# Retention and a bilinear FFN on one core: another order of the tokens, and the third pair in the opening's form

## The chip, the core and the metric

The kernel runs on one core of a Trainium2 chip. The metric is the device time of one execution in microseconds (us). "Median" is the median of the runs named.

TensorE is PE in the profile, its weight loads are PEld, VectorE is DVE, ScalarE is ACT, GpSimd is POOL, and SyncE (SP) issues most transfers.

## The reference, cut to what matters

```python
B, H, S, D = 8, 8, 576, 64                     # 4608 tokens, 512 features
scores = (q @ k.T) / sqrt(D)                   # per batch and head
ret    = scores * gamma_h ** (i - j), 0 where j > i
attn   = ret @ v                               # -> x [4608, 512]
out    = ((x @ w_a) * (x @ w_b)) @ w_out       # d_ff = 1536
```

The decay lets a block of 64 tokens be computed from its own scores and one running state (the sum of k^T v over the earlier blocks of the batch). A batch has nine blocks of 64. Tokens can be worked off in any order as long as the states of a batch come in sequence; each token's FFN row is independent of the others.

## The kernel before

Attention is cut into units that are dropped into gaps between the FFN's matrix products, because the FFN (1,404 products, mostly of 512 columns, 0.216 us each) fills TensorE from about 18 us to the end. There are three forms:

- the *opening*: 512 tokens as 2 pairs of 256 tokens x 2 halves of four heads. A partition holds two neighbouring tokens (512-byte rows in the loads), and the products use the array in quarters of 64x64;
- two single 128-token *chunks* (the third pair, tokens 512 to 767), with 256-byte rows;
- fifteen *pairs* of 256 tokens in quarters, each worked in a *stretch*: outputs from states, a fence (a small ScalarE copy out of the output tile, for which the products that add to this tile must wait), state products (`keyed`), scores (`matched`), outputs from scores.

```python
    def rows_of(i):                      # tokens of chunk i: batches one after the other
        b, m = 2 * (i // PER), i % PER   # PER = 9 chunks for two batches
        if m < MID:
            return [(0, 128, b, 128 * m)]
        if m == MID:                     # this one straddles two batches
            return [(0, 64, b, 128 * m), (64, 64, b + 1, 0)]
        return [(0, 128, b + 1, 64 + 128 * (m - MID - 1))]

    def keyed(n):                        # state products of a stretch
        kvs = [ps_ffn.tile([128, 2, HP, 64], FP32, tag="ab", name=f"kv{a}")
               for a in (0, 1)]          # two of the four PSUM buffers of the FFN
        ...
                for a, r in QUADS:
                    if block_of(n, 2 * kp + a) == BL - 1:
                        continue         # a batch's ninth block feeds no state
                    nc.tensor.matmul(kvs[a][half(r), kp, c, :], ...)
        def add(i):                      # running sums on VectorE
            ...
            elif m < BL - 1:
                nc.vector.tensor_tensor(sums[:, i], own, prev, op=ALU.add)
        later.append(lambda: (add(0), add(1)))   # one entry runs in each gap
        later.append(lambda: (add(2), add(3)))

    def stretch(into, outof):
        flush()
        if outof is not None:
            ...
            from_states(outof, o, begun)
            nc.scalar.copy(fence, o[:, :, 0, kp, 0])   # before from_keys may add
        if into is not None:
            convert, convert_swapped = keyed(into)
            masked = matched(into)
        if outof is not None:
            scaled = from_keys(outof, o, begun)
        ...

    # the last lines of ffn_block: one store for 128 tokens
                    nc.sync.dma_start(out[rows, cols], osb[:, cols])

    # places, counted in FFN products of 512 columns
    for i, places in ((4, (110, 117, 121, 127)), (5, (127, 132, 136, 139))):
        todo += [(at, one_by_one, (what, i))           # the two single chunks
                 for at, what in zip(places, "CTSA")]  # cast, turn, score, output
```

Of the kernel before, what the change touches and what calls it, by code (L numbers as in the profile page):

```python
# [18 lines left out]
def kernel(  # L19
# [21 lines left out]

    NP = NTOK // 256
    BL = S // 64
    FIRST = 3
    PER = 2 * S // 128
    MID = PER // 2
    HALF = S - 128 * MID
    assert HALF == 64 and NTOK % (2 * S) == 0 and BL == 9

    def rows_of(i):  # L50

        b, m = 2 * (i // PER), i % PER
        if m < MID:
            return [(0, 128, b, 128 * m)]
        if m == MID:
            return [(0, 64, b, 128 * m), (64, 64, b + 1, 0)]
        return [(0, 128, b + 1, 64 + 128 * (m - MID - 1))]

# [54 lines left out]
    staged, shared = {}, {}  # L113
# [7 lines left out]

    def load(i):
        tiles = []
        for name, src in (("qf", q), ("kf", k), ("vf", v)):
            t = half_of(stage, i, [DM], FP32, name)
            for r0, n, b, s0 in rows_of(i):
                nc.sync.dma_start(
                    t[r0:r0 + n, :].rearrange("p (h d) -> p h d", h=H),
                    src[b, :, s0:s0 + n, :].rearrange("h s d -> s h d"))
            tiles.append(t)  # L130
        staged[i] = tiles
# [3 lines left out]
    def load_pair(n):  # L135
        if n >= NP:
            return
        paired[n] = []
        for name, src in (("qf", q), ("kf", k), ("vf", v)):
            t = stage.tile([128, 2 * DM], FP32, tag=name, name=name + "2")  # L140
            for kp in (0, 1):
                for r0, m, b, s0 in rows_of(2 * n + kp):
                    nc.sync.dma_start(
                        t[r0:r0 + m, kp * DM:(kp + 1) * DM]
                        .rearrange("p (h d) -> p h d", h=H),
                        src[b, :, s0:s0 + m, :].rearrange("h s d -> s h d"))
            paired[n].append(t)

    def load_step(n, hh, which):

        if n not in paired:
            paired[n] = [stage.tile([128, 2 * DM], FP32, tag=name, name=name)
                         for name in ("qf", "kf", "vf")]
        nc.sync.dma_start(  # L154
            paired[n][which][:, hh * DM:(hh + 1) * DM]
            .rearrange("p (h e) -> p h e", h=4),
            (q, k, v)[which][0, 4 * hh:4 * hh + 4, 256 * n:256 * n + 256, :]
            .rearrange("h (p two) d -> p h (two d)", two=2))

    STEPS = [(0, 0), (1, 0), (0, 1), (1, 1)]  # L160
# [7 lines left out]
    idxp_i = const.tile([128, 6], INT32)  # L168
    nc.gpsimd.iota(idxp_i[:, 0:4], pattern=[[256, 2], [1, 2]], base=0,
                   channel_multiplier=2)  # L170
    for col, base in ((4, 512), (5, 64)):
        nc.gpsimd.iota(idxp_i[:, col:col + 1], pattern=[[1, 1]], base=base,
                       channel_multiplier=1)
# [12 lines left out]
    idxv_i = const.tile([128, BL, 2], INT32)  # L186
    mask = const.tile([128, 128], BF16)
    mask2 = const.tile([128, 128], BF16)
    mask3 = const.tile([128, 64], BF16)

    def make_masks():
        nc.gpsimd.memset(two_states, 0.0)
        nc.gpsimd.iota(idxv_i, pattern=[[256, BL], [128, 2]], base=0,
                       channel_multiplier=1)
        nc.gpsimd.memset(mask, 1.0)
        nc.gpsimd.affine_select(
            out=mask, in_=mask, compare_op=ALU.is_ge, fill=0.0,
            base=0, pattern=[[1, 128]], channel_multiplier=-1)
        nc.gpsimd.tensor_copy(mask2, mask)
        nc.gpsimd.memset(mask2[0:64, 64:128], 0.0)  # L200
# [3 lines left out]
    idxp_f = const.tile([128, 6], FP32)  # L204
    nc.vector.tensor_copy(idxp_f, idxp_i)
    nc.vector.tensor_scalar_add(idxp_f[64:128, 4:5], idxp_f[64:128, 4:5],
                                -float(S))
# [6 lines left out]
    vs = const.tile([128, H, 6], FP32)  # L214
# [4 lines left out]
    qs = const.tile([128, HP, S + 192], FP32)  # L219
    idx_f = qs[:, HP - 1]  # L220
    nc.vector.tensor_copy(idx_f[:, 0:512],
                          idx_o.rearrange("p u k x -> p (u k x)"))

    def make_qs(c, s0, s1):
        nc.scalar.activation(qs[:, c, s0:s1], idx_f[:, s0:s1], AF.Exp,  # L225
                             bias=biasq[:, 0:1], scale=lgp[:, c:c + 1])

    idxv = const.tile([128, BL, 2], FP32)
    wrap = const.tile([128, BL, 2], FP32)
    vs2 = const.tile([128, BL, 2, H], FP32)  # L230

    def pair_tables(step):
        if step == 0:
            nc.gpsimd.tensor_copy(mask3[0:64], mask[0:64, 0:64])
            nc.gpsimd.tensor_copy(mask3[64:128], mask[64:128, 64:128])
            nc.vector.tensor_copy(idxv, idxv_i)
            for _ in range(4):
                nc.vector.tensor_scalar(wrap, idxv, float(S), float(S),
                                        op0=ALU.is_ge, op1=ALU.mult)
                nc.vector.tensor_tensor(idxv, idxv, wrap, op=ALU.subtract)  # L240
        elif step == 5:
            idx_i = sum_pool.tile([128, S + 192], INT32, tag="sums",
# [3 lines left out]
            nc.gpsimd.iota(idx_i[:, S:S + 192], pattern=[[1, 192]], base=0,  # L246
                           channel_multiplier=0)
            nc.vector.tensor_copy(idx_f, idx_i)  # L248
# [4 lines left out]
        else:  # L253
            part = (S + 192) // 2
            s0 = step % 2 * part
            make_qs((step - 6) // 2, s0, s0 + part)

    two_states = state_pool.tile([128, 2, HP, 128], BF16, tag="states",
                                 name="state2")
    states = [two_states[:, i] for i in (0, 1)]  # L260
    state_after = const.tile([128, 2, 2, HP, 128], BF16)
# [13 lines left out]
    natural, transposed, kv_of, state_of, scored = {}, {}, {}, {}, {}  # L275
    state_of[4] = state_after[:, 1, 1]
    sums_of, states_of = {}, {}
# [15 lines left out]

    def half(i):
        return slice(64 * i, 64 * i + 64)
# [21 lines left out]
    def values_step(i, kp, on):  # L317
        n, hh = STEPS[i]
        to, fro = by_parity(natural[n, hh][1])[:, :, kp], given(i, 2)[:, :, kp]
        by = vs[:, 4 * hh:4 * hh + 4, 2 * n + kp]  # L320
# [40 lines left out]
    def state_step(i, behinds):  # L361
# [4 lines left out]
        for behind in behinds:  # L366
            parts = [(0, slice(0, 128))] if n else []
# [14 lines left out]
        which = slice(behinds[0], behinds[-1] + 1)  # L382
        for r in (0, 1):
            nc.scalar.copy(
                state_after[half(r), n, which, 2 * hh:2 * hh + 2, half(r)],
                kv[half(r), which])

    def output_step(i, place=None):
# [5 lines left out]
        else:  # L394
            o = place.tile([128, 2, 512], FP32, tag="sc", name="o0")
        for a in (0, 1):
            if (n, a) == (0, 0):
                continue
            st = state_after[:, 0, 0] if (n, a) == (0, 1) else (
                state_after[:, n - 1 + a, 1 - a])  # L400
# [6 lines left out]
        for j in (0, 1):  # L407
            for kp in (0, 1):
                for a, r in QUADS:
# [5 lines left out]
                        start=((n, a, j, kp) == (0, 0, 0, 0)), stop=True,  # L415
# [3 lines left out]
            x_of(256 * n, 256)[:, cs].rearrange("p j (a s) -> p a j s", a=2),  # L419
            o[:, :, 0:256].rearrange("p a (j s) -> p a j s", j=2),  # L420
            qs[:, cs, 256 * n:256 * n + 256]
            .rearrange("p j (a s) -> p a j s", a=2), op=ALU.mult)

    def cast(i, on="pool"):

        qf, kf, vf = staged.pop(i)
        qkb = half_of(nat, i, [2, DM], BF16, "qkb")
        vb = half_of(nat, i, [DM], BF16, "vb")
        qb, kb = qkb[:, 0], qkb[:, 1]
        if on == "pool":  # L430
            nc.gpsimd.tensor_copy(qb, qf)
        else:
            nc.scalar.copy(qb, qf)
        if on == "dve":
            nc.vector.tensor_copy(kb, kf)
        else:
            nc.gpsimd.tensor_copy(kb, kf)
        nc.gpsimd.tensor_tensor(  # L438
            vb.rearrange("p (h d) -> p h d", h=H),
            vf.rearrange("p (h d) -> p h d", h=H),  # L440
            vs[:, :, i].unsqueeze(2).to_broadcast([128, H, D]),
            op=ALU.mult)
        natural[i] = (qkb, qb, kb, vb)

    def transposes(i):

        natural_qk = natural[i][1:3]
        qkT = half_of(qkt_pool, i, [2, HP, 128], BF16, "qkT")
        for w, copy in ((0, nc.scalar.copy), (1, nc.vector.tensor_copy)):
            tp = ps_ffn.tile([128, HP, 128], BF16, tag="ab", name="tp")  # L450
            for p in range(HP):
                nc.tensor.transpose(tp[:, p, :],
                                    natural_qk[w][:, p * 128:(p + 1) * 128],
                                    identity)
            copy(qkT[:, w], tp)
        transposed[i] = qkT

    def state(i):
        m = i % PER
        if m == PER - 1:  # L460
            return
        qkb, qb, kb, vb = natural[i]
        r = slice(64, 128) if m == MID else slice(0, 128)
        if not kv_of:
            kv_of[0] = ps_o[0].tile([128, HP, 128], FP32, tag="kv",
                                    name="kv")
        kv = kv_of[0]
        for p in range(HP):
            sl = slice(p * 128, (p + 1) * 128)
            nc.tensor.matmul(kv[:, p, :], kb[r, sl], vb[r, sl],  # L470
# [537 lines left out]
```

## Time and profile before

The three runs before the prediction had a median of 334.37 us (333.58 to 334.53). These are lines of the page of the profiled execution: its span, then busy time, share of the span and instruction count of each engine, then the chain of work that ended last, by engine.

```profile
span 332.6 us, 8648 instructions
PE 324.9 (98%) x3612; PEld 167.4 (50%) x3612; DVE 166.8 (50%) x304; ACT 128.7 (39%) x275; POOL 115.3 (35%) x148
...
PE 93%; DVE 2%; DMA 2%; ACT 1%; issue 1%; SPq 0%; POOL 0%; ACTq 0%; DVEq 0%; POOLq 0%
```

TensorE is what bounds the kernel. So a change is worth what it takes from TensorE's products and waits, from the opening before the first FFN product, or from the tail after the last. The view of TensorE's waits (who waited for whom: us in total, times, longest) lists nearly everything that is left there:

```profile
PE w L843 <- DVE ones L203: 1.5, 1, 1.5
PE o L712 <- ACT fence L740: 1.0, 3, 0.4
PE tp L452 <- DVE qkb L435: 0.6, 1, 0.6
PE pa L779 <- DVE xT L539: 0.6, 1, 0.6
```

The last two belong to the single chunks. The timeline of TensorE (start, duration, what, and in brackets the idle time before it) shows the second one: the first product of the first 256-token FFN block waits for VectorE's write of its input.

```profile
53.63 1.04 PE L814 MATMUL po<-wo_sb,hT 128*128 128x512 bf16 x4
55.22 0.60 PE L779 MATMUL pa<-xT,wa_sb 128*128 128x256 bf16 x4 [0.55 <-DVE xT L539]
```

The tail, from the timeline: the last copy on ScalarE, and the issue of the last store by SyncE.

```profile
329.42 0.37 ACT L823 COPY osb<-po 128x256 f32<-128x256 f32 x1 [2.03 <-PE po L814]
329.82 0.33 SPq L831 DMA_DIRECT2D out_dram<-osb  x1
```

### The profile page before, as it was taken

To read this page: it belongs to the slowest core of one execution; us is meant where nothing else is said; L and a number is where in the kernel's file an instruction comes from. 1 tells how busy PE (TensorE), PEld (TensorE's weight loads), DVE (VectorE), ACT (ScalarE), POOL (GpSimd) and SP (SyncE) were. 2 spreads that over 40 slices of the span, in tenths; PEclk is the share of its full clock that TensorE was granted. 3 is DMA by queue.
4 is the path that set the end of the run, shared out by engine and by line. 5 is a ranking of instruction groups with operands and counts; after the bars stand their busy time and mean duration, and the time that the engine had idled before them with its cause. 6 is when DMAs were issued, how large, how long until landed. Compare 5 with 4: busy or idle time off the path is not lost.

```text
span 332.6 us, 8648 instructions
## 1 busy us (share of the span) xinstructions
PE 324.9 (98%) x3612; PEld 167.4 (50%) x3612; DVE 166.8 (50%) x304; ACT 128.7 (39%) x275; POOL 115.3 (35%) x148
## 2 busy tenths in 40 slices
PE   7999998999999999999999999999999999999996
PEld 3744445858644554545454545454545454444443
DVE  6745446456745464566247623762476247414321
ACT  7735743434515344353134323533352334213321
POOL 4890038570557468167045503370340000000000
PEclk9999999999999999999999999999999999999999
DMA  7999999999999999898599259945970420020002
GB/s 211 250 185 206 207 216 213 225 187 191 177 221 231 194 209 252 183 204 153 132 230 209 51 140 193 212 79 143 198 106 2 131 62 0 3 95 32 2 32 95
DMA packets 146151, 50.37 MB, mean 151 GB/s; under 512 B 130624, under 2 KB 141632, under 8 KB 146112
## 3 DMA queue, kind: packets, MB, share of 16 engines
q1 hardware_dynamic: 141360, 45.10, 67.0%
q0 software_dynamic: 4752, 4.72, 8.7%
q8 instruction: 28, 0.46, 0.6%
q14 instruction: 11, 0.09, 0.1%
HBM read 37.75 MB, written 9.44 MB: 142 GB/s over the span
## 4 chain that ended last, share of the span: by engine, by line
PE 93%; DVE 2%; DMA 2%; ACT 1%; issue 1%; SPq 0%; POOL 0%; ACTq 0%; DVEq 0%; POOLq 0%
PE pb L794 28%; PE pa L779 28%; PE po L814 27%; DMA qf<-in_q_dram 2%; PE o L699 2%; PE o L712 1%; PE sc L673 1%; PE kv L622 1%; PE kv L375 1%; PE tp L332 1%; PE w L843 0%; SPq L154 0%; PE pa L761 0%; DVE xT L539 0%; PE sc L347 0%
## 5 line engine op out<-in xcount | busy, mean ns | idle before, releaser
L799 DVE TENSOR_TENSOR hT<-ha,pb 128x512 bf16<-128x512 bf16 (+1 forms) x120 | 76.0, 634 | 97.8 <-PE pb L794 91.2
L787 ACT CAST ha<-pa 128x512 bf16<-128x512 f32 (+1 forms) x120 | 64.8, 543 | 122.8 <-PE pa L779 122.1
L794 PE MATMUL pb<-xT,wb_sb 128*128 128x512 bf16 (+1 forms) x480 | 111.8, 358 | 0.1
L779 PE MATMUL pa<-xT,wa_sb 128*128 128x512 bf16 (+1 forms) x474 | 110.3, 358 | 0.8 <-DVE xT L539 0.6
L814 PE MATMUL po<-wo_sb,hT 128*128 128x512 bf16 (+1 forms) x444 | 97.3, 373 | 0.0
L794 PEld LDWEIGHTS <-wb_sb 128*128 128x128 bf16 x480 | 46.8, 98 | 47.2 <-issue 1.1
L779 PEld LDWEIGHTS <-wa_sb 128*128 128x128 bf16 x474 | 45.3, 98 | 46.6 <-issue 1.9
L814 PEld LDWEIGHTS <-hT 128*128 128x128 bf16 x444 | 42.4, 98 | 47.0
L562 POOL CAST qkb<-qf 64x1024 bf16<-64x1024 f32 x15 | 15.4, 1029 | 84.2 <-DMA qf<-in_q_dram 79.3
L825 DVE COPY osb<-po 128x512 f32<-128x512 f32 (+1 forms) x18 | 12.2, 677 | 44.3 <-PE po L814 44.3
L567 POOL TENSOR_TENSOR vb<-vf,vs 128x1024 bf16<-128x1024 f32 x15 | 28.5, 1901 | 8.6 <-PE o L712 3.1
L823 ACT COPY osb<-po 128x512 f32<-128x512 f32 (+1 forms) x19 | 10.9, 575 | 45.5 <-PE po L814 45.5
L721 DVE TENSOR_TENSOR xT<-o,qs 128x512 bf16<-128x512 f32 x30 | 19.6, 682 | 5.3 <-PE o L712 5.3
L641 DVE TENSOR_TENSOR sums<-kv,sums 128x256 f32<-128x256 f32 x47 | 19.9, 423 | 4.6 <-PE kv L622 3.1
L682 DVE TENSOR_TENSOR sT<-sc,mask 128x512 bf16<-128x512 f32 x30 | 19.8, 681 | 0.0
L562 POOL CAST qkb<-kf 64x1024 bf16<-64x1024 f32 x15 | 15.5, 1033 | 9.5 <-DMA kf<-in_k_dram 9.1
L566 POOL CAST qkb<-qf 64x512 bf16<-64x512 f32 x30 | 17.7, 617 | 0.8 <-issue 0.2
L566 POOL CAST qkb<-kf 64x512 bf16<-64x512 f32 x30 | 17.6, 614 | 0.9
L653 ACT CAST states<-sums 64x512 bf16<-64x512 f32 (+1 forms) x30 | 17.2, 574 | 0.5
L843 PE MATMUL w<-ones 128*128 128x256 bf16 (+1 forms) x36 | 8.2, 354 | 1.5 <-DVE ones L203 1.5
L438 POOL TENSOR_TENSOR vb<-vf,vs 128x512 bf16<-128x512 f32 x2 | 2.1, 1056 | 20.8 <-DMA vf<-in_v_dram 20.8
L225 ACT ACTIVATE qs<-qs,biasq,lgp 128x384 f32<-128x384 f32 (+1 forms) x12 | 8.1, 734 | 2.9 <-DVE qs L248 2.4
(103 smaller groups left out, 160.8 us busy)
## 6 DMA issues: line engine op xcount, KB each, us to landing
qf<-in_q_dram SPq DMA_DIRECT2D x32, 256.0 KB, 4.4
kf<-in_k_dram SPq DMA_DIRECT2D x32, 256.0 KB, 5.3
vf<-in_v_dram SPq DMA_DIRECT2D x32, 256.0 KB, 5.4
out_dram<-osb SPq DMA_DIRECT2D x31, 256.0 KB, 2.2
wo_sb<-in_moe_w_out_dram POOLq DMA_DIRECT2D x3, 512.0 KB, 16.4
out_dram<-osb SPq DMA_DIRECT2D x10, 128.0 KB, 2.4
qf<-in_q_dram SPq DMA_DIRECT2D x8, 128.0 KB, 4.0
kf<-in_k_dram SPq DMA_DIRECT2D x8, 128.0 KB, 5.4
```

The costliest lines, as they stand in the source:

```text
L562: nc.gpsimd.tensor_copy(qkb[0:64, w], t[0:64])
L566: nc.gpsimd.tensor_copy(to[:, :, 1 - r], fro[:, :, r])
L567: nc.gpsimd.tensor_tensor(vb.rearrange("p (k h d) -> p k h d", k=2, h=H), vf.rearrange("p (k h d) -> p k h d", k=2, h=H), vs2[:, n % BL].u ...
L641: nc.vector.tensor_tensor(sums[:, i], own, prev, op=ALU.add)
L653: nc.scalar.copy(into[half(1 - r)].rearrange("p (k a) c d -> p a k (c d)", a=2)[:, 1, which.start // 2: which.stop // 2], sums[half(r)].re ...
L682: nc.vector.tensor_tensor(sT[:, on].rearrange("p c k s -> p (c k) s"), sc[:, on].rearrange("p c k s -> p (c k) s"), mask3.unsqueeze(1).to_ ...
L721: nc.vector.tensor_tensor(x_of(t0, 128).rearrange("p c (a s) -> p c a s", a=2), o[:, :, :, kp].rearrange("p a c s -> p c a s"), qs[:, :, s ...
L779: nc.tensor.matmul(pa[:, 0:n], wa_sb[:, c, fs], xT[:, c], start=(c == 0), stop=(c == NC - 1))
L787: nc.scalar.copy(ha[:, 0:n], pa[:, 0:n])
L794: nc.tensor.matmul(pb[:, 0:n], wb_sb[:, c, fs], xT[:, c], start=(c == 0), stop=(c == NC - 1))
L799: nc.vector.tensor_tensor(hT[:, F, 0:n], has[F][:, 0:n], pb[:, 0:n], op=ALU.mult)
L814: nc.tensor.matmul(po[:, 0:width], hT[:, F, u * 128:(u + 1) * 128], wo_sb[:, F, cols], start=(F == 0), stop=(F == NF - 1))
```

## The change

Intent: no special forms after the opening. The first 512 tokens of each batch are two pairs of four blocks that never straddle a batch, and the last 64 tokens of all eight batches make two pairs at the very end ("left" pairs). The third pair then starts a batch and can take the opening's form: 512-byte rows in its loads and quarters of the array. Masks, tables and code for single chunks go. The core of the diff:

```diff
-        b, m = 2 * (i // PER), i % PER
-        ...
+        if n < LEFT:                                  # LEFT = 16 pairs
+            return [(kp, 0, 128, n // 2, 256 * (n % 2) + 128 * kp)
+                    for kp in (0, 1)]
+        return [(i // 2, 64 * (i % 2), 64, 4 * (n - LEFT) + i, S - 64)
+                for i in range(4)]                    # 4 batches, 64 tokens of each
...
-    def cast(i, on="pool"): ...       # and transposes, state, scores, outputs
...                                    # of single chunks: all gone
     def keyed(n):
+        if n >= LEFT:
+            return (lambda: None,) * 2                # left pairs feed no state
...
-                    if block_of(n, 2 * kp + a) == BL - 1:
-                        continue
...
+    def store(u, cols, osb):
+        n, u = u // 2, u % 2
+        for kp, r0, m, b, s0 in rows_of(n):
+            rows = out[b * S + s0:b * S + s0 + m, cols]
+            if kp != u:
+                continue
+            if n < FIRST:
+                for par in (0, 1):
+                    nc.sync.dma_start(rows[par::2], osb[half(par), cols])
+            else:
+                nc.sync.dma_start(rows, osb[r0:r0 + m, cols])
...
-    load(4)
-    load(5)
+    for i, which in ((4, Q), (4, K), (4, V), (5, Q), (5, K), (5, V)):
+        load_step(*STEPS[i], which)
...
+            (100, early_casts, ()), (112, turn_step, (4,)),
+            (112.1, cast_step, (5, Q, "act")), (116, score_step, (4,)),
+            (124, turn_step, (5,)), (124.1, state_step, (4, (0, 1))),
+            (128, score_step, (5,)), (132, output_step, (4,)),
+            (132.1, state_step, (5, (0, 1))), (140, output_step, (5,))]
```

State products in the stretches: 416 instead of 424, nearly the same work. All other products of the pairs keep their number.

## The prediction

> **What bounds it.** TensorE. The page gives PE 324.9 of 332.6 us busy (98%), mean granted clock 1.000; the chain of waits is 93% PE, 83% of it the three FFN products. In the windows view PE is never idle between 100 and 280 us. The view of waits lists only 3.7 us for PE: 1.5 at the start, 1.0 for the ACT fence, 0.6 for a DVE cast, 0.6 for the DVE write of xT. DVE (50%), ACT (39%) and POOL (35%) are no limits. The input queue is busy for most of the first 150 us, but after the opening no PE wait names a DMA. So only TensorE work, TensorE waits, the opening (first FFN matmul at 18.16 us) and the tail count.
>
> **TensorE work.** Counting instructions: FFN, warm-up and pair products are the same but for 416 instead of 424 64x64 state products (-0.1 us).
>
> The third pair changes from two 128-token chunks to two head halves in quarters. By the timeline the chunks occupy 45.01 to 55.22 us = 10.2 us, of which 24 po matmuls take 24 x 0.216 = 5.2. They cost 5.0 us, with visible waits (DVE cast of kf 0.56, xT 0.55) and hidden ones: the chain of waits has ACT and DVE pieces from 47.1 to 50.3 and from 52.0 to 55.2 us. The same half in the opening takes (chain of waits) 0.45 transposes + 0.42 scores + 0.49 states + 0.46 outputs = 1.8 us; two make 3.6. Their places are spread wider (units 100 to 140, not 110 to 139), casts come earlier, and the loads are 6 DMAs instead of 9, each issued in about 0.65 us: the first half should land by about 41 us, 2 us before PE wants it. Left is perhaps 0.2 us for the last xT at the start of block 1. Gain: 5.0 - 3.8 = **1.2 us**, on the critical path.
>
> **512-byte rows.** The Trainium skill ("DMA: Bandwidth & Descriptors", the table at its head) gives 512 B as the smallest transfer for line rate. But the third pair is 1.5 MB of 50 and no PE wait names its loads; I expect only the earlier landing.
>
> **Tables and masks.** Less DVE, ACT and POOL work (eight DVE operations of 0.18 us, qs 128x320 instead of 128x384, a 1.0 us memset), off the path. The opening's chain runs through an unchanged qf load that lands at 7.5 us: -0.1.
>
> **Tail.** The last two pairs hold 64-token pieces, so each store becomes two DMAs of 64 rows. The last copy ends at 329.8 us and its store is issued in 0.33 us; a second issue follows: **+0.3 us**.
>
> **Sum.** 334.37 - 1.2 - 0.1 - 0.1 + 0.3 = 333.3. Predicted **333.3 us**, range 332.3 to 334.5. Faster by over 2%: 0.01; within 2%: 0.98; slower by over 2%: 0.01.
>
> **What would show it.** First FFN matmul still at about 18.1 us; the first 256-token block starts at about 54.0 us, not 55.2; PE's waits for the cast of kf and for xT vanish or shrink; from there to the last po the distance is unchanged within 0.2 us; from the last po copy to the end of the span about 0.3 us more; packets fall by about 3,000 (1.5 MB in 512- instead of 256-byte rows).
>
> **What would make it wrong.** The third pair's K and value casts all run on POOL (six, about 0.6 us each) behind loads that may land late: then PE waits at unit 112 or 124 and the gain is lost. State copies on ACT or DVE may be late for the second half's outputs. The left pairs' state copies may lengthen the fence waits. The stores in two parts might cost more than an issue at the end.

## The result, and the profile after

The changed kernel took 335.30 us (median of four runs, 334.85 to 335.44) and the kernel before 334.26 us (four runs). The ratio is 1.0032, with a 95% interval of 1.0014 to 1.0050. Ratios are the mean time of one kernel's runs over that of the other's of the same rounds, so not quite the ratio of the medians quoted. The time lies outside the predicted range (332.3 to 334.5), and the sign is wrong: 1.0 us was lost where 1.1 us had been expected to be won.

The page after:

```profile
span 333.7 us, 8670 instructions
PE 322.0 (96%) x3611; PEld 167.7 (50%) x3648; DVE 162.8 (49%) x292; ACT 128.0 (38%) x275; POOL 114.6 (34%) x146
...
PE 93%; issue 2%; DMA 2%; ACT 1%; DVE 1%; SPq 0%; ACTq 0%; DVEq 0%
```

Beware of one thing: only 3,611 products are recorded for 3,648 weight loads. Where a product's record is missing, the page shows idle time with "issue" as its reason. TensorE's waits after, with 2.4 us of such false idle time on the second and fourth lines:

```profile
PE w L723 <- DVE ones L186: 1.5, 1, 1.5
PE po L699 <- issue: 1.4, 9, 0.2
PE o L584 <- ACT fence L613: 1.0, 3, 0.4
PE pa L664 <- issue: 1.0, 6, 0.2
PE tp L305 <- DVE qkb L288: 0.5, 1, 0.5
```

Both waits of the single chunks are gone; the wait of 0.5 us in the last line belongs to the opening, where it did not end up as time: c1 below, the same kernel again, does not have it and reaches its first FFN weights no earlier (18.13 us against 18.15). The first 256-token block starts at 54.39 us, as the prediction said (54.0), and not at 55.22 us:

```profile
53.74 0.81 PE L699 MATMUL po<-wo_sb,hT 128*128 128x512 bf16 x3 [0.16 <-issue]
54.39 0.60 PE L664 MATMUL pa<-xT,wa_sb 128*128 128x256 bf16 x4
```

The tail is what stands out. From the timeline, the last copy and the two stores that follow it (the first is issued at 330.00 us, the second ends its issue at 331.18 us):

```profile
329.53 0.37 ACT L708 COPY osb<-po 128x256 f32<-128x256 f32 x1 [2.04 <-PE po L699]
330.00 0.55 SPq L637 DMA_DIRECT2D out_dram<-osb  x1
330.60 0.59 SPq L637 DMA_DIRECT2D out_dram<-osb  x1
```

Weight loads are all recorded in each trace, so they make reliable milestones. The table cuts the spans at three of them: A, the first weights of the FFN; B, the first weights of the first 256-token block's *output* product (so the third pair and what waits for it lie before B); C, the last weights of the kernel. It was computed from the traces and covers the experiments too.

| kernel (profiled execution) | start to A | A to B | B to C | C to end | span |
|---|---|---|---|---|---|
| before | 17.97 | 49.89 | 261.14 | 3.56 | 332.56 |
| changed | 18.15 | 48.89 | 262.07 | 4.63 | 333.74 |
| c1_after_again | 18.13 | 48.88 | 261.75 | 4.61 | 333.37 |
| e1_one_store | 18.29 | 48.88 | 262.09 | 17.81 | 347.07 |
| b1_split_store | 18.13 | 49.66 | 261.25 | 4.77 | 333.81 |
| e3_old_third | 18.08 | 49.58 | 261.66 | 4.78 | 334.10 |
| e2_two_queues | 17.80 | 48.89 | 261.69 | 4.17 | 332.54 |
| e5_sums_at_once | 17.96 | 48.98 | 261.92 | 4.62 | 333.48 |
| b2_full_states | 17.63 | 49.85 | 262.06 | 3.54 | 333.08 |
| e4_256_rows | 18.09 | 49.01 | 264.45 | 4.77 | 336.32 |
| e6_fence_apart | 17.58 | 48.89 | 260.98 | 4.61 | 332.06 |
| e7_all_three | 17.55 | 48.89 | 260.13 | 4.18 | 330.75 |
| e8_turns_earlier | 17.82 | 48.88 | 260.20 | 4.18 | 331.08 |
| b3_before_same_mends | 17.51 | 49.70 | 261.51 | 3.54 | 332.26 |

Names that begin with b are made from the kernel before, the others from the changed one. Changed minus before: +0.18 up to A, -1.00 from A to B, +0.93 from B to C, +1.07 after C; together +1.18 us, the difference of the spans. So the gain that was predicted did arrive, before B, and was given back twice, in two places where the prediction had put -0.1 and +0.3 us.

### The profile page after: what moved, and what is told of

The parts are those of the page before. It is cut to its first block, busy times and chain, and to the rows that moved or that the text cites. A ratio compares the mean times of both kernels' runs of the same rounds, so it can differ in the third digit from the quotient of the medians.

```text
span 333.7 us, 8670 instructions
## 1 busy us (share of the span) xinstructions
PE 322.0 (96%) x3611; PEld 167.7 (50%) x3648; DVE 162.8 (49%) x292; ACT 128.0 (38%) x275; POOL 114.6 (34%) x146
## 4 chain that ended last, share of the span: by engine, by line
PE 93%; issue 2%; DMA 2%; ACT 1%; DVE 1%; SPq 0%; ACTq 0%; DVEq 0%
PE pb L679 28%; PE po L699 28%; PE pa L664 27%; PE o L584 2%; DMA vf<-in_v_dram 2%; PE o L571 2%; PE sc L545 1%; PE kv L489 1%; PE kv L348 1%; PE tp L305 1%; PE sc L320 1%; PE o L398 1%; PE w L723 1%; PE pa L646 0%; ACT ha L672 0%
## 5 line engine op out<-in xcount | busy, mean ns | idle before, releaser
L664 PE MATMUL pa<-xT,wa_sb 128*128 128x512 bf16 (+1 forms) x458 | 108.2, 357 | 1.6 <-issue 1.0
L699 PE MATMUL po<-wo_sb,hT 128*128 128x512 bf16 (+1 forms) x430 | 95.2, 373 | 1.7 <-issue 1.4
L513 ACT CAST states<-sums 64x512 bf16<-64x512 f32 x26 | 16.0, 617 | 0.4
L288 POOL CAST qkb<-kf 128x512 bf16<-128x512 f32 x5 | 3.1, 614 | 19.0 <-DMA kf<-in_k_dram 19.0
L584 PE MATMUL o<-sT,vb 64*64 64x64 bf16 x480 | 7.1, 195 | 1.2 <-ACT fence L613 1.0
```

Of the source, the lines that this page charges most:

```text
L513: nc.scalar.copy(to(half(1 - r)), fro(half(r)))
L664: nc.tensor.matmul(pa[:, 0:n], wa_sb[:, c, fs], xT[:, c], start=(c == 0), stop=(c == NC - 1))
L699: nc.tensor.matmul(po[:, 0:width], hT[:, F, u * 128:(u + 1) * 128], wo_sb[:, F, cols], start=(F == 0), stop=(F == NF - 1))
```

## The experiments

Twelve kernels ran, in three groups, each with five rounds of timing beside the kernel before on the same chip (c1, e1, b1, e3; then e2, e5, b2, e4; then e6, e7, e8, b3; each group on another chip; medians of the kernel before: 334.50, 334.69 and 334.17 us). All gave the right result.

### c1_after_again: what repeats

No edit.

> The changed kernel once more, unchanged, to tell what repeats. If the pieces of the difference are properties of the program, this trace again has the first FFN weights at 18.15 us, the first 256-token block's first product at about 54.4 us, a pause of 0.15 us in the third and seventh 512-token-order blocks (near 100.9 and 241.9 us), a stretch of 1.9 us at 122 us, and 3.8 us from the last copy to the end of the span; time 335.3 us. If the opening (+0.2 us) and the stretch at 122 us (+0.4 us) are chance, such as a late instruction fetch or a late load, they come back by 0.1 us or more different.

Measured: 335.26 us (ratio 1.0023, interval 0.9992 to 1.0053). A to B and the tail repeat within 0.02 us. The stretch at 122 us came back 0.28 us shorter, so B to C is 261.75 us: of the +0.93, about 0.3 was chance and 0.6 is the program's (0.5 by e2 and e3 below, whose stretches are the same). The start up to A does not go with the order of the tokens: over the kernels made from the one before it is 17.51 to 18.13 us, over those made from the changed one 17.55 to 18.29. It goes with the group of runs instead: 18.08 to 18.29 us in the four traces of the first group, 17.63 to 18.09 in the second, 17.51 to 17.82 in the third, with kernels of both orders in each. The landing of the first V load does not explain it: that was at 6.33 us in the trace before, at 6.88 us in the changed one, and at 6.16 us in c1, which still reached A at 18.13 us.

Where in B to C the program's part lies can be read from the traces: all kernels load the same FFN weights in the same order, so the distance between two such loads can be compared one by one. Against the kernel before, c1 loses 0.15 us in each of two new pauses (100.9 and 241.6 us), 0.14 us in the stretch at 122 us, 0.17 us in that at 238 us and small pieces of up to 0.04 us in others, and wins 0.13 and 0.03 us in the two stretches that take states for no pair (254 and 271 us); together +0.60 us.

### e1_one_store: one store of 128 rows for two batches

```diff
+        if n >= LEFT:
+            b = 4 * (n - LEFT) + 2 * u
+            nc.sync.dma_start(
+                out.rearrange("(b s) m -> b s m", s=S)[b:b + 2, S - 64:, cols],
+                osb[:, cols])
+            return
```

> The changed kernel with the two 64-row stores of each 128-row tile of the last four 128-token tiles of each left pair merged into one store of 128 rows with a two-batch address pattern. Theory: the tail's extra 1.0 us is the second issue (0.58 us) and the longer first (0.55 instead of 0.33 us), so the distance from the last copy to the end of the span falls from 3.8 to about 2.8 us, and the time from 335.3 to about 334.3 us. Rival: the address pattern with two batches, not the number of stores, is what is slow; then the one store is issued in about 1.1 us and the tail stays at 3.7 us or more, time 335.2.

Measured: 348.29 us, ratio 1.040 (1.037 to 1.043). The rival named the right thing, the address pattern with two batches, but by far too little: the tail became 17.8 us. The store's issues (count, then ns min/median/max) and the DMA traffic of the window from 320 to 348 us in 40 slices, in GB/s:

```profile
L631 SPq DMA_DIRECT2D out_dram<-osb x5: 512/672/4942, 322.5 to 332.6; - x5
GB/s 0 0 0 0 0 23 26 32 29 35 53 53 53 47 53 53 53 47 53 53 53 47 53 53 47 53 53 53 47 50 48 48 47 50 47 50 41 0 0 0
```

The stores crawl at 53 GB/s. Summing the durations of the packets in any microsecond of that window gives 2.1 engines at work; for the kernel before, the 144 packets of a 256 KB store sum to 11 engine-microseconds within one microsecond. The Trainium skill tells why ("DMA: Bandwidth & Descriptors", section "Why a DMA increments its semaphore by 16 and not by 1", and its rules for kernel authors): the number of engines is the largest that divides the slowest dimension of both patterns, and "an outermost dim of size c < 16 [...] confines the whole DMA to at most c engines". The outermost dimension here is 2, and 2.1 is what the trace shows. So two stores of 64 rows are the better of these two ways, and the run tells nothing about the cost of the second issue.

### b1_split_store: the kernel before with its last stores cut in two

```diff
+                elif tok0 + u * 128 >= NTOK - 512:
+                    for k in (0, 1):
+                        nc.sync.dma_start(
+                            out[rows.start + 64 * k:rows.start + 64 * k + 64,
+                                cols], osb[half(k), cols])
```

> The kernel before with only the stores of the last 512 tokens cut into two of 64 rows each. Theory of the issue cost: the distance from the last copy to the end of the span grows from 2.8 to 3.8 us and the time from 334.3 to 335.3 us, nothing else moves. Rival (the scattered addresses of the new order are slow): here the addresses stay contiguous, so the tail grows only by one issue of 0.33 us, to 3.1 us, time 334.6.

Measured: 335.35 us (ratio 1.0038, 0.9995 to 1.0081: the interval just includes 1, as one run was 339.7 us). The trace is plain: C to end is 4.77 us instead of 3.56 us, and nothing else moved by more than 0.25 us. The addresses are contiguous here, so scattered addresses are not the cause; two stores of 64 rows are. The issue of the ten half stores (ns min/median/max):

```profile
L832 SPq DMA_DIRECT2D out_dram<-osb x10: 467/566/589, 322.3 to 330.5; - x10
```

A store of 128 rows was issued in 0.33 us when nothing delayed it, one of 64 rows takes 0.47 to 0.59 us: half the rows, and a longer issue. Why it is longer is not shown.

### e2_two_queues: the second half store from ScalarE's queue

```diff
-                nc.sync.dma_start(rows, osb[r0:r0 + m, cols])
+                on = nc.scalar if n >= LEFT and r0 else nc.sync
+                on.dma_start(rows, osb[r0:r0 + m, cols])
```

> The changed kernel with the second 64-row store of each tile of the left pairs issued from ScalarE's queue instead of SyncE's. Theory: the tail's 1.0 us is two issues of about 0.55 us one after the other on one queue; side by side, about 0.6 us of it goes: last copy to end of span 3.8 becomes about 3.2 us, time 335.3 becomes 334.7 us. Rival: the 64-row transfers themselves are slow (each row's packet takes 0.15 us instead of 0.085 us) and the landing after the last issue gets later by as much; then the tail stays within 0.2 us of 3.8 us.

Measured: 334.62 us, ratio 0.9998 (0.998 to 1.0017). C to end fell from 4.6 to 4.17 us, B to C stayed (261.69). The two issues now lie side by side:

```profile
329.19 0.47 SPq L638 DMA_DIRECT2D out_dram<-osb  x1
329.20 0.50 ACTq L638 DMA_DIRECT2D out_dram<-osb  x1
```

Not quite half of the tail's loss is won back, a little less than expected (0.45 of 0.6 us). The skill says the same of two queues (same page, "Issuing engines are not separate DMA queues"): they "only save the time on the sequencer it takes to initiate the DMA, which is usually small relative to the DMA itself". Here nothing lies behind the last store to hide it, so it counts in full.

### e3_old_third: the third pair in the old form

The single chunks' functions and places come back for the third pair; it starts a batch here, so its first chunk needs no state and neither straddles a batch.

```diff
-    for i, which in ((4, Q), (4, K), (4, V), (5, Q), (5, K), (5, V)):
-        load_step(*STEPS[i], which)
+    ps_next("ps_chunk")
+    load(4)
+    load(5)
...
-            (100, early_casts, ()), (112, turn_step, (4,)),
-            ...
+    for i, places in ((4, (110, 117, 121, 127)), (5, (127, 132, 136, 139))):
+        todo += [(at, one_by_one, (what, i))
+                 for at, what in zip(places, "CTSA")]
```

> The changed kernel with its third pair in the old form: two single 128-token chunks, 256-byte rows, placed where the kernel before has them; all else as in the changed kernel. Theory 1: the form of the third pair is what brought the first 256-token block forward (from 37.1 to 36.0 us after the first FFN product), so here its first product waits for xT again and starts at about 55.2 to 55.4 us, and the time is 0.8 to 1.0 us longer than the changed kernel's, about 336.2 us. Theory 2: lighter tables and masks, or the earlier loads of the pairs, did it; then the block starts at about 54.5 us and the time is 335.3 us.

Measured: 335.73 us, 0.47 us above the changed kernel in the same rounds. A to B goes from 48.88 to 49.58 us, so 0.70 us of the third pair's gain belongs to its form, and the wait for its input is back:

```profile
55.02 0.60 PE L805 MATMUL pa<-xT,wa_sb 128*128 128x256 bf16 x4 [0.55 <-DVE xT L539]
```

Theory 1 holds, but its size was too large: 0.70 us in the trace and 0.47 us in the medians, where 0.8 to 1.0 us had been expected. In four traces of kernels with the old order A to B is 49.66 to 49.89 us, mean 49.78; so the whole gain before B is 0.9 us on average (48.89 after), and about 0.2 us of it is not the form. The chunks of the old order straddle two batches and both read states; whether that is the 0.2 us was not tested apart.

### e4_256_rows: the third pair with 256-byte rows

```diff
+        if n == FIRST - 1:
+            for two in (0, 1):
+                nc.sync.dma_start(
+                    paired[n][which][:, hh * DM:(hh + 1) * DM]
+                    .rearrange("p (h two d) -> p h two d", h=4, two=2)[:, :, two],
+                    (q, k, v)[which][n // 2, 4 * hh:4 * hh + 4, 0:256, :]
+                    .rearrange("h (p two) d -> p h two d", two=2)[:, :, two])
+            return
```

> The changed kernel with its third pair's loads cut into 256-byte rows (12 loads instead of 6), layout in the array unchanged. If longer rows matter to the time, TensorE waits for the casts of the second half and the first 256-token block starts later than 54.4 us by some tenths, time 335.6 us or more. If only the landing moves (about 1.3 instead of 0.9 us for each 256 KB, so the last one about 2 us later than 44.3 us) and no product waits for it, the time stays within 0.2 us of 335.3.

Measured: median 335.15 us, as the changed kernel; A to B 49.01 us, 0.13 us more. So the longer rows matter little to TensorE before B. They do matter to the queue: in the changed kernel the third pair's six loads of 256 KB land 0.9 us apart (39.70 to 44.26 us), in the kernel before the first six, of 128 KB each, landed about 0.7 us apart (39.36 to 42.88 us), and the next three, of 256 KB each, 1.2 us apart (44.01 to 46.41 us). The skill's 512 bytes as the smallest transfer for line rate (same page, "Specifications") agrees with that direction.

Two of the six runs took 337.4 and 338.1 us, and the profiled one was the latter. It shows where such a run loses its time: TensorE waits for a transposing DMA of a later pair.

```profile
PE sc L553 <- DMA qkT<-qkb: 1.9, 2, 1.4
```

Runs 1.8 to 4.1 us above the median occur with the kernel before too (three of twelve in the first group), and a wait for a transposing DMA also stands in the traces of e5 and b3, so this run does not show that the shorter rows cause them; that stays open.

### b2_full_states: the kernel before with full stretches

```diff
-                    if block_of(n, 2 * kp + a) == BL - 1:
-                        continue
...
-            elif m < BL - 1:
+            else:
```

> The kernel before with the state product and the running sum of a batch's ninth block done too, though nobody reads them (the result stays right): seven stretches get 32 instead of 24 products and four instead of three sums, as every stretch but the last two has in the changed kernel. Theory: from the second 256-token block to the last product the changed kernel lost 0.55 us because its stretches are all full; here the pauses near 101.5 and 241.8 us appear (0.15 us each), the stretch at 237.9 us goes from 1.49 to 1.67 us, and the time is 0.5 to 0.8 us longer than the kernel before. Rival: the loss is due to addresses or placement of the new order; then the time changes by less than 0.2 us.

Measured: 335.16 us, ratio 1.0021 (1.0000 to 1.0042), so 0.5 us more than the kernel before in these rounds; in the trace B to C is 262.06 instead of 261.14 us. Pauses of 0.15 us appear at 101.3 and 242.0 us as expected, and one more at 275.9 us. (The lengthening to 1.69 us came in the stretch at 204 us and not, as expected, in that at 238 us, which went to 1.56 us.) The weights of the *b* product show the pause: four loads in one row in the kernel before, one and then three in b2.

```profile
241.41 0.74 PEld L794 LDWEIGHTS <-wb_sb 128*128 128x128 bf16 x4
```

```profile
241.59 0.10 PEld L792 LDWEIGHTS <-wb_sb 128*128 128x128 bf16 x1
241.96 0.53 PEld L792 LDWEIGHTS <-wb_sb 128*128 128x128 bf16 x3 [0.27 <-issue]
```

So work that nobody reads, in stretches that used to leave it out, brings on both new pauses of the changed kernel (0.30 us), 0.04 us in front of the first of them, and 0.07 us each in the stretches at 122 and 238 us. That is 0.5 of the 0.6 us that repeat: full stretches are the cause of most of it. The other 0.1 us of the stretch at 238 us (0.17 in c1, 0.07 here) is not explained. That the totals of b2 and the changed kernel are so alike is in part luck: b2 does 56 products more, and 0.4 us of its 0.92 us lie at 204 us, at 271 us and in the third pause, where the changed kernel lost next to nothing.

Why the total count did not show it: the changed kernel has 416 state products against 424, but they are all in thirteen of the pairs, and the two left pairs have none. Thirteen full stretches pay; the stretches without state products win little of it back. At 253.8 us the stretch went from 1.53 us of TensorE's time (120 small products) to 1.40 (96), at 271.5 us from 1.49 to 1.46, because a gap of 0.19 and 0.25 us opens in front of the outputs, where the state products used to lie; it is the place of the fence.

### e5_sums_at_once: all four sums in the first gap

```diff
-        later.append(lambda: (add(0), add(1)))
-        later.append(lambda: (add(2), add(3)))
+        later.append(lambda: (add(0), add(1), add(2), add(3)))
+        later.append(lambda: None)
```

> The changed kernel with the four running sums of a stretch's state products done by VectorE in the first gap instead of two and two. Theory: the pauses of 0.15 us in front of the second weights of the b product two F steps after a stretch (five of them: near 100.9, 139.7, 173.6, 207.5, 241.6 us) are TensorE waiting for the PSUM buffer of the second state product, which the third and fourth sum set free; then all five are gone and the time falls by about 0.7 us to 334.5. Rival: they are instruction fetches or the like; then they stay where they are, and the time too.

Measured: 335.27 us, no gain in time; but all five pauses of 0.15 us are gone, so they are no instruction fetches. The weights that b2 shows split come in one row again:

```profile
241.43 0.74 PEld L679 LDWEIGHTS <-wb_sb 128*128 128x128 bf16 x4
```

In the trace of c1 the pause looks like this (timeline of PEld, PE and DVE):

```profile
240.80 0.69 DVE L684 TENSOR_TENSOR hT<-ha,pb 128x512 bf16<-128x512 bf16 x1 [1.51 <-PE pb L679]
...
241.18 0.10 PEld L679 LDWEIGHTS <-wb_sb 128*128 128x128 bf16 x1
241.41 0.88 DVE L509 TENSOR_TENSOR sums<-kv,sums 128x256 f32<-128x256 f32 x2
241.54 0.81 PE L679 MATMUL pb<-xT,wb_sb 128*128 128x512 bf16 x3
241.55 0.53 PEld L679 LDWEIGHTS <-wb_sb 128*128 128x128 bf16 x3 [0.27 <-issue]
```

The b product's first weights are in at 241.28 us, but it starts at 241.54 us, right after VectorE's product of the *previous* F step (128 of the 1536 columns) ends (240.80 + 0.69 = 241.49). Not, as the theory had it, after the third and fourth sum, which are still running: two of the four PSUM buffers are held by the state products until those sums, and so the FFN has only two left and must wait for its own last evacuation. In e5 the same product begins at 241.64 us while that VectorE product runs until 241.74 us. That TensorE is short of buffers is read from these times; the allocator's choice itself is not in the trace.

The time did not fall since two other waits grew: in the 256-token blocks the longer row of sums comes between VectorE's FFN products, and at 137 us TensorE waited 0.7 us for a transposing DMA (whether the sums bring this on is not shown):

```profile
PE sc L545 <- DMA qkT<-qkb: 0.7, 1, 0.7
PE pb L679 <- DVE sums L509: 0.2, 1, 0.2
```

### e6_fence_apart: the fence with FFN products behind it

Where a stretch takes in no new pair, the outputs from states and the fence move one gap (4 or 8 products) ahead.

```diff
+    todo += [(at - (4 if at < starts[3] + 144 else 8), open_up, (args[1],))
+             for at, fn, args in todo if fn is stretch and args[0] is None]
```

> The changed kernel with the state products of the three stretches that take in no new pair (pairs 3, 5 and 17 going out) and their fence moved ahead of the stretch, by one gap between FFN products (4 or 8 products). Theory: these stretches hold TensorE 0.48 to 0.56 us each on ScalarE's fence copy because nothing lies between; apart, the wait is gone but each costs one more change between large and small products (about 0.3 us in the other short groups), so 0.1 to 0.3 us is won on each, time 335.3 becomes 334.7. Rival: the extra change of form costs as much as the wait; then the time stays within 0.2 us.

Measured: 334.14 us, ratio 0.9992 (0.9970 to 1.0014). B to C is 0.77 us shorter than in c1 (260.98 against 261.75), and the fence's 1.0 us is gone from TensorE's list of waits. In the timeline, first c1 with the wait, then e6 with four FFN products in its place:

```profile
69.80 0.45 PE L571 MATMUL o<-qkT,states 64*64 64x64 bf16 x32
70.61 0.45 PE L584 MATMUL o<-sT,vb 64*64 64x64 bf16 x32 [0.36 <-ACT fence L613]
```

```profile
68.39 0.45 PE L571 MATMUL o<-qkT,states 64*64 64x64 bf16 x32
68.77 1.04 PE L709 MATMUL po<-wo_sb,hT 128*128 128x512 bf16 x4
69.74 0.45 PE L584 MATMUL o<-sT,vb 64*64 64x64 bf16 x32
```

### e7_all_three, e8_turns_earlier, b3_before_same_mends: repairs together

e7 is e6 with e2's two queues and e5's sums, those only from pair 6 on, where the FFN blocks are 512 tokens wide:

```diff
+        first = (0, 1) if n < 6 else (0, 1, 2, 3)
+        later.append(lambda: [add(i) for i in first])
+        later.append(lambda: [add(i) for i in range(len(first), 4)])
```

> The changed kernel with three repairs: left stores on two queues (0.5 us), the four sums at once from pair 6 on, where the blocks are 512 tokens wide (0.6 us), fences apart (0.6 us). If the pieces add up, 335.3 - 1.7 = 333.6 us, about 0.9 us below the kernel before. If the sums at once only move the wait to another place, as in the run where that was done everywhere (a wait of 0.7 us for a transposing DMA near 137 us), 334.2 us or more.

Measured: 332.93 us (332.47 to 333.74), ratio to the kernel before 0.9960 (0.9938 to 0.9982). That is 1.2 us below the kernel before in the same rounds, where 0.9 had been expected. B to C is 260.13 us, 1.6 us below c1, the tail 4.18 us, and TensorE's list of waits has one line left:

```profile
PE w L735 <- DVE ones L186: 1.5, 1, 1.5
```

e8 also places the later casts and transposing DMAs 8 products earlier.

```diff
-        casts[n], turns[n] = placed[n] - 70, placed[n] - 38
+        casts[n], turns[n] = placed[n] - 78, placed[n] - 46
```

> The kernel with the three repairs, and the casts and transposing DMAs of pairs 9 to 17 placed 8 products earlier. If the waits for the transposing DMA seen near 137 us in two runs come from too little time between issue and use, they vanish and the scatter of the times shrinks, 333.4 us; if the DMA queue is simply full then, nothing changes or it gets worse, since the loads behind them move too.

Measured: 333.19 us (332.79 to 335.42, ratio 0.9972). Nothing is won and the scatter is not smaller. As neither profiled execution had such a wait, the run does not tell what causes them.

b3 is the kernel before with the same two repairs in its stretches (sums from pair 6 on, fences apart).

> The kernel before with the same two repairs in its stretches (sums at once from pair 6, fences apart), to tell whether they or the new order make a faster kernel. The sums can win 0.45 us here (three pauses), the fences 0.6: 334.5 becomes 333.5 us. If the new order with its third pair in the opening's form is worth something by itself, the repaired changed kernel is 0.3 us or more below this one; if not, they are equal.

Measured: 333.96 us (333.19 to 334.60), ratio 0.9984 (0.9962 to 1.0005). The repaired changed kernel is 1.0 us below it, more than the 0.8 us that A to B differ by (49.70 against 48.89); b3's profiled execution also lost 1.2 us to a transposing DMA. So the repairs alone do not make the faster kernel. How much of the 1.0 us is the new order's own is not settled: without that one wait the profiled spans would differ by 0.3 us (332.26 - 1.2 against 330.75), since the two stores still cost the new order 0.6 us in the tail, and whether the wait goes with the old order was not tested.

## Why the prediction was wrong, point by point

- **TensorE bounds the kernel; loads, tables and masks do not matter.** Right. Packets fell by 2,959 as said (about 3,000), and e4 shows that the rows' length is hardly felt before B (0.13 us).
- **Third pair: "Gain: 5.0 - 3.8 = 1.2 us".** Right in mechanism: both waits vanished, and B came earlier. The size was 0.9 us on average (1.0 against the one trace it was computed from); of it e3 shows 0.7 for the form.
- **Tail: "a second issue follows: +0.3 us".** This term was mis-sized most, a risk that the prediction names itself ("The stores in two parts might cost more than an issue at the end"). It took the 0.33 us of a store of 128 rows for one of 64 rows. In the trace: the first issue begins 0.10 instead of 0.03 us after the last copy, since SyncE is still busy with the pair of stores before (+0.07); the two issues last 1.18 us instead of one of 0.33 (+0.85); landing and finish are 0.15 us longer. Together +1.07 us, and b1 brought +1.2 us with nothing but the cut. The right number was in the profile of before, in the 64-row stores of the opening's tokens (ns min/median/max):

```profile
L828 SPq DMA_DIRECT2D out_dram<-osb x8: 542/596/1195, 57.3 to 69.9; - x8
```

- **"FFN, warm-up and pair products are the same but for 416 instead of 424 64x64 state products (-0.1 us)".** This step failed, and with it "from there to the last po the distance is unchanged within 0.2 us". The count was right and the conclusion was not: +0.6 us that repeats (c1), and 0.3 us more by chance in the first trace. The kernel before skipped one block in seven of its stretches, which shortened them and in two of them kept the FFN out of a shortage of PSUM buffers (pauses of 0.15 us; b2 brings them on, e5 takes them away). The changed kernel skips everything in two stretches instead, where the fence's latency then lies bare and only 0.16 us is won. About 0.1 us of the 0.6 stays unexplained.
- **Opening: -0.1.** Nothing was won that could be told from chance (17.5 to 18.3 us in either kernel).

With the measured sizes the sum is -0.9 + 0.6 + 1.1 = +0.8 us. In the rounds of c1 the medians differ by 335.26 - 334.50 = 0.76 us.

## What to carry to other kernels

Read the cost of an added instruction from one of the same shape in the trace, not from its larger neighbour: a store of half the rows took longer to issue, and at the end of a kernel every issue counts in full. When work is moved and its total stays, ask what each place loses and what each place gains: leaving out products helps where a buffer or the time is short, and wins little where they only covered a wait. If a change pays in one place and costs in two, measure the places separately and mend them: here three small repairs turned +0.8 us into -1.2 us. Not all of that mends the change: the fences (0.8 us) and three of the five pauses are in the kernel before as well.

## What the Trainium skill lacked or had wrong

- "DMA: Bandwidth & Descriptors" calls the time to initiate a DMA "usually small relative to the DMA itself" and has no figure for it by shape. Here SyncE's issue took 0.33 us for a store of 128 rows and 0.47 to 0.59 us for one of 64 rows of the same length, and cutting the stores in two cost 1.1 to 1.2 us at the end of the kernel (changed kernel, b1).
- The same page's rules advise against two transfers to disjoint halves of the partitions and for one of 128 partitions. When the halves go to two places in memory, the one transfer got the outermost dimension 2 and ran on 2.1 engines: 348.3 instead of 335.3 us (e1). The rule on the outermost dimension on that page foretells it; the advice on halves does not mention the exception.
- "TensorEngine Tiling (Array Packing)", section "Tiling Modes", says that changing the tiling mode drains TensorE, without a figure. In the traces a group of 32 products in quarters set between FFN products delays the FFN by 0.48 us (e6: the first FFN weights come 0.68 us later than without it, and the next follow them 0.20 us sooner), and a group of 64 delays it by 0.77 us, counted in the same way (c1, the stretch at 63 us). So 32 products more cost 0.29 us, and an estimate from these two leaves about 0.2 us for going in and out.
- No page was found to tell that, in a profile, matrix products may be missing while their weight loads are there (the NOTIFIC pages speak of dropped records in general): 3,611 against 3,648 in the changed kernel, shown as 2.4 us of idle time that did not exist.
